# A build-time planner gets PSUM places and DMA queue times; filter products merged; x loads held

## The chip, the cores and the metric

One core of a Trainium2 chip. The metric is the device time of one execution in microseconds (us), less is better. The kernel before takes 312.05 us (median of three runs, 311.57 to 312.36).

The core has a matrix engine (PE, whose weight loads are the row PEld), two evacuating engines (DVE, the vector engine, and ACT, the scalar engine), POOL (GpSimd) and SP (the sync engine); POOL and SP here mainly issue DMAs. Each engine runs its own instructions strictly in order and waits on semaphores.

## The reference

Eight batches of 3200 x 256 values pass a global filter and then a gated unit:

```python
X = np.fft.rfft(x, axis=1)
y = np.fft.irfft(X * (filt_r + 1j * filt_i)[None], n=3200, axis=1)
xp = np.concatenate([np.zeros((B, 4, D)), y], axis=1)
gate_pre = sum(conv_w[k] * xp[:, k:k + S, :] for k in range(5))
out = (1 / (1 + np.exp(-gate_pre)) * (y @ w_val)) @ w_out
```

Input and output are float32; the kernel works in bf16 and fp16 with float32 accumulation.

## The kernel before

The length 3200 is split into 100 x 32, so that both transforms are two short matrix stages with a transposition between them. Every batch goes through the same pieces. The names are those of the planner's tasks, and the number of pieces per batch stands behind each.

- lx (8): POOL issues the load of a part of x (200 KB by the profile's list of issues) into one of ten buffers, converting to bf16 (line 168).
- s1 (8): PE, first transform stage (line 434). so (8): its evacuation from PSUM, on ACT or DVE.
- t (4): DVE transposes 32 x 32 blocks, tile `tt` (line 453). All eight so must be done.
- s2 (7): PE, second stage (line 463); xs (7): its evacuation.
- z (2 x 7): DVE multiplies xs by the real and by the imaginary filter part, `za` and `zb` (line 481).
- ia (7): PE, first inverse stage (line 494); ue (7): its evacuation into `u`.
- For batch 0, k (4): DVE transposes `u` into `vt` (line 535). For the other batches SP writes `u` to DRAM (wr, 7, line 517) and reads it back turned (lv, 8, lines 527 and 528).
- ib (8): PE, second inverse stage (line 545); ye (8): its evacuation on ACT (line 554) into `yt`.
- cv, ga, vl, gv, op, oe, st (7 each): convolution on PE as products with diagonal matrices (line 576), sigmoid on ACT (line 586), value product on PE (line 595), gate times value on DVE (line 610), output product on PE (line 618), its evacuation into `o` on ACT or DVE, and the store issued by SP (line 633).

At the start the transform tables are computed (iota, sine), the filter is loaded in two halves by POOL (lines 228 to 234) and doubled onto other partitions by SP (line 259), and the diagonal matrices `dg_t` are made on DVE (line 410).

**The order.** Nothing is scheduled at run time. The class `Plan` runs once when the kernel is built. Every piece is a task with costs for the engines that can do it, a rank, and tasks that it depends on; counted rooms (buffers) are taken and given back. `Plan.run` steps through an imagined time: whenever an engine is free, the ready task with the lowest rank goes next. PE changes between 64x64 and full tiles carry a penalty `stay`, and a task that both ACT and DVE could do carries `lean` on DVE. The list it returns is the order in which the instructions are emitted, and so the order in which each engine runs them. Its costs decide nothing but that order; on the chip each instruction waits for what it really needs.

PSUM is four tiles of [128, 1024] float32 from a pool that hands them out in turn:

```python
    def psum():
        return pp.tile([128, 1024], FP32, name="ps", tag="ps")
```

The plan counts them as one room (`ps=4`). x loads have the DMA queue as a task of 1.35 each ("DQ"), the spill and the stores have only fixed landing times.

Of the kernel before, what the change touches and what calls it, by code (L numbers as in the profile page):

```python
# [19 lines left out]
NM = 13  # L20
NV = 4 * NS
TURN = (0,)
RC = 4
# [4 lines left out]
MAGIC = 12582912.0  # L28


class Plan:
# [3 lines left out]
    def __init__(self, room, stay=1.0, lean=0.0):  # L35
        self.tasks, self.room, self.stay = {}, dict(room), stay
        self.lean = lean

    def add(self, name, engines, rank, deps, emit, take=(), give=(), land=0.0, mode=None):
        self.tasks[name] = dict(engines=engines, rank=rank, deps=deps, emit=emit, take=take,  # L40
                                give=give, land=land, mode=mode)

    def run(self):
# [8 lines left out]
        mode = None  # L52
# [4 lines left out]
        while left:  # L57
            gives.sort()
            while gives and gives[0][0] <= now + 1e-9:
                for pool in gives.pop(0)[1]:  # L60
                    self.room[pool] += 1
            best = None
            for n in ready:
# [23 lines left out]
            for p in t["take"]:  # L87
                self.room[p] -= 1
            if e == "PE":
                if t["mode"] != mode:  # L90
                    cost += 0.1
                mode = t["mode"]
            end = now + cost
            free[e] = end
            if t["give"]:
                gives.append((end + 0.1, t["give"]))
            for u in users.get(n, ()):
                need[u] -= 1
                ready_at[u] = max(ready_at[u], end + 0.1 + t["land"])
                if need[u] == 0:  # L100
                    ready.add(u)
            order.append((t["emit"], e))
# [5 lines left out]
def kernel(  # L108
# [36 lines left out]
    fr_t = cpool.tile([128, 2, NM, D], BF16, name="fr_t")  # L145
    fi_t = cpool.tile([128, 2, NM, D], BF16, name="fi_t")
# [5 lines left out]
    pp = ctx.enter_context(tc.tile_pool(name="ps", bufs=4, space=bass.MemoryType.PSUM))  # L152
# [6 lines left out]

    def psum():  # L160
        return pp.tile([128, 1024], FP32, name="ps", tag="ps")

    st = {}
# [39 lines left out]
    def pool_setup():  # L203
# [18 lines left out]
        for m0, m1 in FCUT:  # L222
            nm = m1 - m0
            for f, dst in ((filt_r, fr_t), (filt_i, fi_t)):
# [24 lines left out]
    def sp_setup():  # L249
# [5 lines left out]
        for m0, m1 in FCUT:  # L255
            for dst in (fr_t, fi_t):
                for t in range(2):
                    p = 64 * t
                    nc.sync.dma_start(out=dst[p + 32:p + 64, :, m0:m1, :],
                                      in_=dst[p:p + 32, :, m0:m1, :])  # L260
# [146 lines left out]
    def diag():  # L407
        for r in range(2):
            rows = slice(64 * r, 64 * r + 64)
            V.tensor_tensor(  # L410
                dg_t[rows].rearrange("p h k j -> p (h k) j"),
                g["ident"][rows, 64 * r:64 * r + 64].unsqueeze(1)
                .to_broadcast((64, 2 * K, 64)),
                g["cw"][rows].rearrange("p h k -> p (h k)").unsqueeze(2)
                .to_broadcast((64, 2 * K, 64)), op=ALU.mult)

    NGB, NOB = 3, 3
# [58 lines left out]
    def zed(b, u, which, e):  # L476
        m0, nm = UCH[u]
        xs_ = st["XS", b, u]
        z = zpool.tile([128, 2, 2 * D], BF16, name="za" if which == 0 else "zb")
        f = (fr_t, fi_t)[which]  # L480
        (nc.vector if e == "DVE" else nc.gpsimd).tensor_tensor(  # L481
            z[:, :, 0:nm * D], xs_[:, :, 0:nm * D],
            f[:, :, m0:m0 + nm, :].rearrange("p h m d -> p h (m d)"), op=ALU.mult)
        st["Z", b, u, which] = z

    def inva(b, u):
        m0, nm = UCH[u]
        zz = [st.pop(("Z", b, u, w)) for w in range(2)]
        ps = psum()
        for a in range(nm):  # L490
            for w, tab in enumerate((a_t, b_t)):
                for t, h in ((0, 0), (1, 1), (0, 1), (1, 0)):
# [4 lines left out]
                        rhs=zz[w][rows, h, D * a:D * a + D],  # L497
# [132 lines left out]
    def store(b, c):  # L630
# [7 lines left out]
    plan = Plan(dict(ps=4, xt=NXT, so=1, t=1, xs=3, za=3, zb=3, u=1, e=2, v=1, y=2, g=NGB,  # L638
                     gv=NGB, o=NOB), stay=1.5, lean=2)
# [4 lines left out]

    for b in range(B):
        t0 = NCH * b
        for j in range(NCH):
            if b:
                add(f"lx{b},{j}", {"POOL": 0.6}, t0 + j - 9, ["pool"],
                    lambda e, b=b, j=j: load_x(b, j), take=("xt",), land=1.5)  # L650
                add(f"dx{b},{j}", {"DQ": 1.35}, t0 + j - 9, [f"lx{b},{j}"], None, land=2.0)
            dep = [f"dx{b},{j}"] if b else [f"x0{j}", "cfa"]
            dep = dep + ([f"s1{b},{j - 1}"] if j else [])
            add(f"s1{b},{j}", {"PE": 0.45}, t0 + j, dep, lambda e, b=b, j=j: s1(b, j),
                take=("ps",) + (("so",) if j == 0 else ()), give=("xt",), mode=0)
            add(f"so{b},{j}", two(0.93, 1.14), t0 + j, [f"s1{b},{j}"],
                lambda e, b=b, j=j: so(b, j, e), give=("ps",))
        for q in range(4):
            add(f"t{b},{q}", {"DVE": 1.14}, t0 + NCH + 1.5, [f"so{b},{j}" for j in range(NCH)]
# [3 lines left out]
        for u, (m0, nm) in enumerate(UCH):  # L663
            r = t0 + NCH + 1 + u
            half = 0 if m0 + nm <= FCUT[0][1] else 1
            add(f"s2{b},{u}", {"PE": 0.14 * nm}, r, ["wa"] + [f"t{b},{q}" for q in range(4)]
                + ([f"s2{b},{u - 1}"] if u else []),
                lambda e, b=b, u=u: s2(b, u), take=("ps", "xs", "za", "zb"),
                give=("t",) if u == len(UCH) - 1 else (), mode=1)
            add(f"xs{b},{u}", two(0.13 + 0.4 * nm, 0.04 + 0.55 * nm), r, [f"s2{b},{u}"],  # L670
                lambda e, b=b, u=u: xs(b, u, e), give=("ps",))
            for w in range(2):
                add(f"z{w}{b},{u}", {"DVE": 0.06 + 0.27 * nm}, r, [f"xs{b},{u}", f"fl{half}"] + (
                    [f"z0{b},{u}"] if w else []),
                    lambda e, b=b, u=u, w=w: zed(b, u, w, e), give=("xs",) if w else ())
            add(f"ia{b},{u}", {"PE": 0.25 * nm}, r + 1.5, [f"z0{b},{u}", f"z1{b},{u}", f"te{u // 2},1", f"pd{b}"],
                lambda e, b=b, u=u: inva(b, u), take=("ps",), give=("za", "zb"), mode=1)
            add(f"ue{b},{u}", two(0.13 + 0.4 * nm, 0.04 + 0.55 * nm), r + 1.5, [f"ia{b},{u}", f"pd{b}"],
                lambda e, b=b, u=u: ue(b, u, e), give=("ps",))
        turned = b in TURN  # L680
        every = [f"ue{b},{u}" for u in range(len(UCH))]
        add(f"pd{b}", {"POOL": 1.2} if turned else {"none": 0.0}, t0 + NCH - 2,
            ["pool"] + ([f"pd{b - 1}"] if b else []),
            lambda e, b=b: pad(b), take=("u",) if turned else ("u", "e"))
        if turned:
            for q in range(4):
                add(f"k{b},{q}", {"DVE": 1.14}, t0 + NCH + 13, every
# [3 lines left out]
        else:  # L691
            for u in range(len(UCH)):
                r = t0 + NCH + 1 + u
                add(f"wr{b},{u}", {"SP": 0.45}, r + 1.5, [f"ue{b},{u}"],
                    lambda e, b=b, u=u: wr(b, u))
                add(f"wl{b},{u}", {"none": 0.0}, r + 1.5, [f"wr{b},{u}"], None, land=3.0)
            add(f"wd{b}", {"none": 0.0}, r + 1.5, [f"wl{b},{u}" for u in range(len(UCH))], None,
                take=("v",), give=("u",))
            for j in range(NCH):
                add(f"lv{b},{j}", {"SP": 0.8}, t0 + NCH + 13 + j, [f"wd{b}"],  # L700
                    lambda e, b=b, j=j: lv(b, j), land=3.5)
        for j in range(NCH):
            r = t0 + NCH + 11.5 + j
            got = f"k{b},3" if turned else f"lv{b},{j}"
            add(f"ib{b},{j}", {"PE": 0.37}, r, [got, "cim"] + ([f"ib{b},{j - 1}"] if j else []),
                lambda e, b=b, j=j: ib(b, j),
                take=("ps",) + (("y",) if j == 0 else ()),
                give=(("v",) if turned else ("v", "e")) if j == NCH - 1 else (), mode=0)
            add(f"ye{b},{j}", {"ACT": 0.77}, r, [f"ib{b},{j}"], lambda e, b=b, j=j: ye(b, j),
                give=("ps",))  # L710
        add(f"ha{b}", {"POOL": 0.2}, t0 + NCH + 11.5, [f"ye{b},0"], lambda e, b=b: halo(b))
        for c in range(NB):
            r = t0 + NCH + 18 + c * 1.3
            f = width(c) / BLK
            add(f"cv{b},{c}", {"PE": 1.03 * f + 0.05}, r,
                [f"ye{b},{j}" for j in range(NCH)] + [f"ha{b}", "dg"],
                lambda e, b=b, c=c: conv(b, c), take=("ps", "g"), mode=1)
            add(f"ga{b},{c}", {"ACT": 0.77 * f + 0.16}, r, [f"cv{b},{c}"],
                lambda e, b=b, c=c: gate(b, c), give=("ps",))
            add(f"vl{b},{c}", {"PE": 0.86 * f}, r, [f"cv{b},{c}"] + ([f"vl{b},{c - 1}"] if c else []),  # L720
                lambda e, b=b, c=c: val(b, c),
# [75 lines left out]
```

## Time and profile before

| | us |
|---|---|
| median of the runs shown | 312.05 |
| the profiled execution, its own time | 313.69 |
| its span, first to last instruction | 311.8 |
| busy PE / DVE / ACT / POOL | 267.2 / 260.7 / 252.8 / 57.8 |
| mean granted PE clock | 0.967 of full |
| DMA bytes | 67.45 MB, mean 216 GB/s |

The profile is one execution. Times that follow are us from the span's start. "Busy" of neighbouring instructions overlaps a little, so that the distance from one start to the next is shorter than the duration shown. A row "A <- B" under the waits says that engine A stood idle until B had finished. In the table of stretches every line gives the start and end, the length, the busy time of PE, PEld, DVE, ACT and POOL with the number of instructions in brackets, the granted clock, the mean busy share of the 16 DMA engines and GB/s. In the timeline a line gives the start, the time taken, the engine, the kernel's line, the operation, what it writes and reads, and in brackets the idle time before it and what ended it.

### The profile page before, as it was taken

How to read it: one execution, taken by the hardware profiler on the slowest of the kernel's cores; microseconds unless marked ns; L12 is line 12 of the kernel's file. 1: busy time of each engine (PE TensorE's matmuls, PEld its weight loads, DVE VectorE, ACT ScalarE, POOL GpSimd, SP SyncE). 2: the span in 40 equal slices, each digit the busy share in tenths (PEclk: the TensorE clock that was granted, in tenths of full speed). 3: DMA queues.
4: the chain of work that ended last, by engine and by line, in shares of the span. 5: the costliest groups of instructions: out<-in, count | busy, mean ns of one | idle time of the engine just before them, and what ended most of it. 6: DMA issues, size and time to landing. Idle time of an engine off the chain costs nothing.

```text
span 311.8 us, 8932 instructions
## 1 busy us (share of the span) xinstructions
PE 267.2 (86%) x3684; PEld 160.2 (51%) x3684; DVE 260.7 (84%) x339; ACT 252.8 (81%) x294; POOL 57.8 (19%) x119
## 2 busy tenths in 40 slices
PE   2815770886999999999999999999999999999992
PEld 0204130254466746665666566656665666666551
DVE  7698689899799989998999899989998985553342
ACT  3945580699699999999999999999999889688762
POOL 8676572230212022102210220000000000000000
PEclk9999996598999999999999999999999999999997
DMA  6999999597799979998999799776566875754444
GB/s 96 178 168 183 209 124 177 76 179 197 179 241 242 269 224 238 311 285 240 249 313 272 226 248 312 245 243 210 177 237 221 244 264 204 260 204 185 167 177 180
DMA packets 53209, 67.45 MB, mean 216 GB/s; under 512 B 7792, under 2 KB 34032, under 8 KB 53168
## 3 DMA queue, kind: packets, MB, share of 16 engines
q1 hardware_dynamic: 41264, 51.79, 50.2%
q0 software_dynamic: 11904, 15.08, 30.7%
q8 instruction: 29, 0.48, 0.6%
q14 instruction: 12, 0.10, 0.1%
HBM read 42.08 MB, written 38.14 MB: 257 GB/s over the span
## 4 chain that ended last, share of the span: by engine, by line
PE 60%; DVE 14%; ACT 9%; DMA 9%; issue 4%; POOL 2%; DVEq 0%; ACTq 0%; POOLq 0%
PE ps L576 17%; PE ps L595 12%; PE ps L618 11%; PE ps L434 7%; PE ps L494 6%; DMA xt<-in_x_dram 6%; DVE gv L610 5%; PE ps L545 4%; DMA fi_t<-in_filt_i_dram 4%; ACT yt L554 3%; PE ps L463 3%; DVE so L427 2%; ACT o L425 2%; ACT u L425 2%; DVE vt L535 2%
## 5 line engine op out<-in xcount | busy, mean ns | idle before, releaser
L610 DVE TENSOR_TENSOR gv<-ps,gt 128x1024 bf16<-128x1024 f32 (+1 forms) x56 | 61.3, 1105 | 27.7 <-ACT gt L586 14.0
L576 PE MATMUL ps<-yt,dg_t 64*64 64x512 bf16 (+1 forms) x1120 | 65.1, 361 | 2.3 <-ACT yt L554 1.6
L586 ACT ACTIVATE gt<-ps 128x1024 bf16<-128x1024 f32 (+1 forms) x56 | 52.1, 934 | 11.0 <-PE ps L576 8.4
L554 ACT ACTIVATE yt<-ps 128x800 bf16<-128x800 f32 x64 | 53.6, 843 | 6.6 <-PE ps L545 5.9
L168 POOL DMA_DIRECT2D xt<-in_x_dram x64 | 35.5, 557 | 119.9 <-PE ps L434 110.3
L434 PE MATMUL ps<-xt,cf_t 100*128 100x512 bf16 x128 | 46.2, 450 | 11.8 <-DMA xt<-in_x_dram 8.7
L618 PE MATMUL ps<-wo_t,gv 128*128 128x256 bf16 x400 | 52.3, 273 | 1.4 <-DVE gv L610 1.2
L595 PE MATMUL ps<-yt,wv_t 128*128 128x512 bf16 (+1 forms) x224 | 52.4, 357 | 0.0
L425 ACT ACTIVATE so<-ps 128x1024 bf16<-128x1024 f32 x40 | 40.8, 1024 | 10.3 <-PE ps L434 7.5
L425 ACT ACTIVATE u<-ps 128x1024 bf16<-128x1024 f32 (+1 forms) x46 | 43.2, 958 | 2.9 <-PE ps L494 2.7
L425 ACT ACTIVATE o<-ps 128x1024 f32<-128x1024 f32 (+1 forms) x44 | 40.8, 938 | 5.2 <-PE ps L618 4.4
L618 PEld LDWEIGHTS <-gv 128*128 128x128 bf16 x400 | 35.8, 97 | 17.0 <-DVE gv L610 7.0
L425 ACT ACTIVATE xs<-ps 128x1024 bf16<-128x1024 f32 (+1 forms) x32 | 29.5, 931 | 17.4 <-PE ps L463 17.2
L576 PEld LDWEIGHTS <-dg_t 64*64 64x64 bf16 x1120 | 32.0, 107 | 22.0 <-issue 6.2
L453 DVE STREAM_TRANSPOSE tt<-so 128x1024 f32<-128x1024 f32 x32 | 38.5, 1227 | 0.6 <-ACT so L425 0.6
L463 PE MATMUL ps<-tt,w_t 64*64 64x256 bf16 x416 | 23.2, 297 | 18.4 <-DVE tt L453 17.5
L481 DVE TENSOR_TENSOR zb<-xs,fi_t 128x1024 bf16<-128x1024 bf16 (+1 forms) x56 | 35.4, 642 | 0.6 <-DMA fi_t<-in_filt_i_dram 0.4
L481 DVE TENSOR_TENSOR za<-xs,fr_t 128x1024 bf16<-128x1024 bf16 (+1 forms) x56 | 35.2, 643 | 0.7 <-ACT xs L425 0.5
L427 DVE CAST so<-ps 128x1024 bf16<-128x1024 f32 x24 | 28.8, 1219 | 7.5 <-PE ps L434 7.5
L545 PEld LDWEIGHTS <-vt 104*128 104x128 bf16 (+1 forms) x512 | 28.9, 98 | 10.6 <-issue 1.9
L545 PE MATMUL ps<-ci_t,vt 104*128 104x100 f16 (+1 forms) x512 | 33.3, 209 | 0.6 <-DVE u L427 0.5
L494 PE MATMUL ps<-za,a_t 64*64 64x256 bf16 x416 | 28.5, 290 | 2.9 <-DVE za L481 1.6
(93 smaller groups left out, 212.3 us busy)
## 6 DMA issues: line engine op xcount, KB each, us to landing
out_dram<-o SPq DMA_DIRECT2D x48, 512.0 KB
xt<-in_x_dram POOLq DMA_DIRECT2D x64, 200.0 KB, 6.4
escr<-u SPq DMA_DIRECT2D x42, 256.0 KB
vt<-escr SPq DMA_DIRECT2D x56, 192.0 KB
out_dram<-o SPq DMA_DIRECT2D x8, 128.0 KB
escr<-u SPq DMA_DIRECT2D x7, 128.0 KB
vt<-escr SPq DMA_DIRECT2D x56, 16.0 KB
fr_t<-fr_t SPq DMA_DIRECT2D x2, 224.0 KB
```

The source lines that it names most:

```text
L425: nc.scalar.activation(dst, src, AF.Copy, **kw)
L434: nc.tensor.matmul(ps[:, 512 * h:512 * h + 512], lhsT=cf_t[0:L].rearrange("p h c i -> p (h c i)"), rhs=xv[:, DQ // 2 * h:DQ // 2 * h + DQ ...
L453: nc.vector.transpose(dst, src)
L481: (nc.vector if e == "DVE" else nc.gpsimd).tensor_tensor(z[:, :, 0:nm * D], xs_[:, :, 0:nm * D], f[:, :, m0:m0 + nm, :].rearrange("p h m d ...
L494: nc.tensor.matmul(ps[64 * h:64 * h + 64, 512 * t + D * a:512 * t + D * a + D], lhsT=tab[rows, h, m0 + a, :], rhs=zz[w][rows, h, D * a:D * ...
L545: nc.tensor.matmul(ps[:, o:o + L], lhsT=v[rows, RC * j + a, 128 * dh:128 * dh + 128], rhs=ci_t[rows, way, :], start=True, stop=True)
L554: nc.scalar.activation(y[:, :, H:H + N].rearrange("p h (a r) -> p h a r", r=R)[:, :, :, RC * j:RC * j + RC], ps[:, :].rearrange("p (h n) - ...
L576: nc.tensor.matmul(ps[64 * dh:64 * dh + 64, 512 * r:512 * r + w], lhsT=dg_t[rows, dh, k, :], rhs=y[rows, dh, BLK * c + k:BLK * c + k + w], ...
L586: nc.scalar.activation(g[:, :, 0:w], two_banks(ps, w), AF.Sigmoid)
L595: nc.tensor.matmul(ps[:, 512 * eh:512 * eh + w], lhsT=wv_t[:, dh, 128 * eh:128 * eh + 128], rhs=y[:, dh, H + BLK * c:H + BLK * c + w], sta ...
L610: nc.vector.tensor_tensor(o, i0, i1, op=ALU.mult)
L618: nc.tensor.matmul(ps[:, D * a:D * a + D], lhsT=gv_[:, eh, 128 * a:128 * a + 128], rhs=wo_t[:, eh, :], start=(eh == 0), stop=(eh == 1))
```

## The change

The planner gets explicit PSUM places, a DMA queue that all transfers share, new costs and new ranks; the kernel gets a merged filter product, diagonal matrices made on ACT, five output buffers and a hold before the later x loads. The order on every engine changes nearly everywhere.

1. PSUM is one tile with four places; a task takes a free place chosen by the plan, which is emitted as written, and the evacuating task gives it back.
2. Spill writes, spill reads and stores pass the task engine "DQ" with costs of their own (0.38 per column, 0.6, 1.2; an x load 1.15). "DQ" takes the task that was ready first and alternates between x loads and the rest.
3. Ranks: `at(stage, n, b)` = 8b + LAG + STEP x n, and FIRST for batch 0, in place of hand-set offsets; `stay` 17.5 and `lean` 12 in place of 1.5 and 2.
4. One z of up to 2048 elements replaces za and zb: xs is read twice through a step of 0, both filter parts stand in one tile `f_t`.
5. `dg_t` is made by ten small ACT instructions, early; the inverse tables (`cid`) wait for batch 0's last t.
6. A one-column copy on POOL reads the last filter column (`hold`); the x loads of batches 1 to 7 and the weight loads depend on it.
7. Output buffers: 3 to 5.

```diff
-    def add(self, name, engines, rank, deps, emit, take=(), give=(), land=0.0, mode=None):
+    def add(self, name, engines, rank, deps, emit, take=(), give=(), land=0.0, mode=None,
+            ps=0, free=()):
...
+    def places(self, n):
+        if n == 0:
+            return []
+        if n == 1:
+            alone = [p for p in self.slots if p ^ 1 not in self.slots]
+            return (alone or self.slots)[:1] or None
...
-                if any(self.room[p] < 1 for p in t["take"]):
+                if self.places(t["ps"]) is None or any(self.room[p] < 1 for p in t["take"]):
...
+                        if e == "DQ":
+                            key = (ready_at[n] + (1e4 if t["mode"] == turn else 0.0), 0.0)
...
+            t["slots"] = self.places(t["ps"])
+            for p in t["slots"]:
+                self.slots.remove(p)
...
+            done = end + SEM.get(e, 0.1)
+            back = list(t["give"]) + [p for o in t["free"] for p in self.tasks[o]["slots"]]
...
+    f_t = cpool.tile([128, 2, 2, NM, D], BF16, name="f_t")
...
+    ps_all = pp.tile([128, 4, 1024], FP32, name="ps")
...
     def psum():
-        return pp.tile([128, 1024], FP32, name="ps", tag="ps")
+        return ps_all[:, st["slots"][0], :]
...
-    def diag():
...
+    def diag(h):
+        for k in range(K):
+            nc.scalar.activation(dg_t[:, h, k, :], g["j2"][:, 0, :], AF.Copy,
+                                 scale=g["cw"][:, h, k:k + 1])
+
+    def gate_loads():
+        hold = g1.tile([128, 1], BF16, name="hold")
+        nc.gpsimd.tensor_copy(hold[...], f_t[:, 1, 1, NM - 1, 0:1])
+
+    NGB, NOB = 3, 5
...
+    def zed(b, u):
+        m0, nm = UCH[u]
+        z = zpool.tile([128, 2, 2, 2 * D], BF16, name="z")
+        nc.vector.tensor_tensor(
+            z[:, :, :, 0:nm * D],
+            st.pop(("XS", b, u))[:, :, 0:nm * D].unsqueeze(1)
+            .to_broadcast((128, 2, 2, nm * D)),
+            f_t[:, :, :, m0:m0 + nm, :].rearrange("p w h m d -> p w h (m d)"), op=ALU.mult)
...
+    def dma(name, us, rank, dep, give=(), land=2.0):
+        add(name, {"DQ": us}, rank, dep, None, land=land, mode=0)
+        add(name + "+", {"none": 0.0}, rank, [name], None, give=give)
...
+        def at(stage, n=0, b=b, t0=t0):
+            return t0 + LAG[stage] + (FIRST.get(stage, 0) if b == 0 else 0) + STEP.get(stage, 1) * n
...
-                add(f"lx{b},{j}", {"POOL": 0.6}, t0 + j - 9, ["pool"],
+                add(f"lx{b},{j}", {"POOL": 0.6}, at("lx", j), ["hold"],
                     lambda e, b=b, j=j: load_x(b, j), take=("xt",), land=1.5)
-                add(f"dx{b},{j}", {"DQ": 1.35}, t0 + j - 9, [f"lx{b},{j}"], None, land=2.0)
+                add(f"dx{b},{j}", {"DQ": 1.15}, at("lx", j), [f"lx{b},{j}"], None, land=2.0, mode=1)
...
-    add("cid", {"DVE": 4.5}, 9, ["wd"], lambda e: ci_dve())
+    add("cid", {"DVE": 4.5}, 13, ["t0,3"], lambda e: ci_dve())
...
-    add("dg", {"DVE": 3.2}, 10, ["t0,3"], lambda e: diag())
+    for h in range(2):
+        add(f"dg{h}", {"ACT": 1.1}, 10, ["ey"], lambda e, h=h: diag(h))
+    add("hold", {"POOL": 0.2}, 0, ["fl1", "pd0"], lambda e: gate_loads())
```

What the new plan puts out for the first batches, against the old one (PE's order, piece by piece, from batch 0's fifth ia on):

```
before: ia0.4 s11.5 s20.6 s11.6 ia0.5 s11.7 ia0.6 s21.0 s12.0 s21.1 s12.1 ib0.0 s12.2 s21.2 ... ib0.7 ia1.5 ia1.6 cv0.0
after:  ia0.4 ia0.5 ia0.6 s11.0 s11.1 ... s11.7 ib0.0 ib0.1 ... ib0.7 s12.0 s21.0 s12.1 s21.1 s12.2 s21.2 s12.3 cv0.0
```

On DVE the four k of batch 0 stand ahead of the four t of batch 1; before they alternated.

More of the change, by code (lines that the diff above doesn't have):

```diff
@@ L51, in run @@
         free = {}
-        mode = None
+        mode = turn = None
         gives = []
@@ L223, in pool_setup @@
             nm = m1 - m0
-            for f, dst in ((filt_r, fr_t), (filt_i, fi_t)):
+            for f, dst in ((filt_r, f_t[:, 0]), (filt_i, f_t[:, 1])):
                 for t in range(2):
@@ L474, in xs @@
         st["XS", b, u] = xs_
-    def zed(b, u, which, e):
+    def zed(b, u):
         m0, nm = UCH[u]
[L478 to L484, printed above, removed]
+        z = zpool.tile([128, 2, 2, 2 * D], BF16, name="z")
[4 more added lines that the diff above has]
+            f_t[:, :, :, m0:m0 + nm, :].rearrange("p w h m d -> p w h (m d)"), op=ALU.mult)
+        st["Z", b, u] = z
     def inva(b, u):
         m0, nm = UCH[u]
-        zz = [st.pop(("Z", b, u, w)) for w in range(2)]
+        z = st.pop(("Z", b, u))
         ps = psum()
@@ L662 @@
                 give=("so",) if q == 3 else ())
[L663 to L679, printed above, removed]
@@ L685 @@
         if turned:
             for q in range(4):
-                add(f"k{b},{q}", {"DVE": 1.14}, t0 + NCH + 13, every
+                add(f"k{b},{q}", {"DVE": 1.87}, at("k"), [f"ue{b},{u}" for u in range(len(UCH))]
                     + ([f"k{b},{q - 1}"] if q else []),
@@ L691 @@
         else:
[L692 to L698, printed above, removed]
+            add(f"wd{b}", {"none": 0.0}, at("ue"), [f"wq{b},{u}+" for u in range(len(UCH))],
+                None, take=("v",), give=("u",))
@@ L732 @@
-    add("pool", {"none": 0.0}, -100, [], None, land=22.0)
-    add("wts", {"POOL": 8.0}, 8.5, ["pool"], lambda e: load_w())
+            add(f"cv{b},{c}", {"PE": 1.08 * f}, at("cv", c),
+                [f"ye{b},{j}" for j in range(NCH)] + [f"ha{b}", "dg0", "dg1"],
+                lambda e, b=b, c=c: conv(b, c), ps=1, take=("g",), mode=1)
+            add(f"ga{b},{c}", {"ACT": 0.77 * f + 0.16}, at("ga", c), [f"cv{b},{c}"],
+                lambda e, b=b, c=c: gate(b, c), free=[f"cv{b},{c}"])
+            add(f"vl{b},{c}", {"PE": 0.87 * f}, at("vl", c),
+                [f"cv{b},{c}"] + ([f"vl{b},{c - 1}"] if c else []), lambda e, b=b, c=c: val(b, c),
+                ps=1, take=("gv",), give=("y",) if c == NB - 1 else (), mode=0)
```

162 lines of the change are left out of this document (90 added, 72 removed).

## The prediction

> **What bounds the kernel now.** I read four views in this order: the slices (where are engines idle), the stretches (which engine fills a batch), the waits (who holds the idle ones), the timeline (what the holder does). "b.n" below is batch b, piece n; s1, so, t, s2, xs, z, ia, ue, ib, ye, cv, ga, vl, gv, op, oe are the planner's task names.
>
> ```profile
> PE   2815770886999999999999999999999999999992
> DVE  7698689899799989998999899989998985553342
> ACT  3945580699699999999999999999999889688762
> PEclk9999996598999999999999999999999999999997
> ```
>
> A slice is 7.8 us. The first 78 us are full of holes on PE and ACT, from slice 11 to 30 all three engines are full, and the last ten slices leave only PE full.
>
> ```profile
> 46.00:56.00 10.00, 0.32 (x8) 0.19 (x8) 10.00 (x8) 0.15 (x1) 3.09 (x6) 0.64 0.95 163
> 108.00:139.70 31.70, 30.89 (x454) 19.63 (x451) 30.36 (x35) 29.89 (x36) 4.54 (x9) 1.00 0.93 262
> 139.70:171.30 31.60, 30.93 (x456) 19.66 (x454) 30.13 (x35) 29.84 (x36) 4.54 (x9) 1.00 0.96 267
> 265.00:308.00 43.00, 41.30 (x509) 24.56 (x507) 19.78 (x19) 30.35 (x35) 0.10 (x1) 1.00 0.53 197
> ```
>
> Columns: stretch, length, then busy us of PE, PEld, DVE, ACT, POOL, granted clock, DMA share, GB/s. The reader is to see three regimes: 46 to 56, DVE alone works; 108 to 234, one batch per 31.6 us with PE, DVE and ACT all over 94% busy and the DMA engines at 0.93 to 0.96; from 265 PE alone.
>
> ```profile
> PE ps L463 <- DVE tt L453: 17.5, 2, 10.2
> ACT xs L425 <- PE ps L463: 17.2, 4, 10.2
> ```
>
> Ten of these us are the hole at 46, and the timeline names it:
>
> ```profile
> 45.70 1.25 DVE L453 STREAM_TRANSPOSE tt<-so 128x1024 f32<-128x1024 f32 x1 [0.59 <-ACT so L425]
> 46.87 1.87 DVE L535 STREAM_TRANSPOSE vt<-u 128x1024 f32<-128x1024 f32 x1
> 48.64 1.20 DVE L453 STREAM_TRANSPOSE tt<-so 128x1024 f32<-128x1024 f32 x1
> ```
>
> DVE turns batch 1's input (L453) and batch 0's output (L535) alternately, eight transposes in 12 us, and PE and ACT can start neither batch until nearly all are done.
>
> **Prices from rows.** Busy times of neighbours overlap, so I take start-to-start distances in the full stretch: DVE evacuation of 1024 elements or a gv 1.14 us, tt 1.16, vt 1.79, za or zb 0.60 (0.31 for the half piece); ACT evacuation 0.92, yt 0.73; PE s1 0.45, s2 0.23, ia 0.44, ib 0.36, cv 1.08, vl 0.87, op 0.88 a piece, about 0.1 at each change between 64x64 and full tiles. These rows give it:
>
> ```profile
> 179.18 1.28 DVE L481 TENSOR_TENSOR za<-xs,fr_t 128x1024 bf16<-128x1024 bf16 x2
> 180.38 0.68 DVE L481 TENSOR_TENSOR zb<-xs,fi_t 128x1024 bf16<-128x1024 bf16 x1
> 180.98 1.22 DVE L610 TENSOR_TENSOR gv<-ps,gt 128x1024 bf16<-128x1024 f32 x1
> 198.52 0.38 DVE L481 TENSOR_TENSOR za<-xs,fr_t 128x512 bf16<-128x512 bf16 x1
> 198.82 1.23 DVE L453 STREAM_TRANSPOSE tt<-so 128x1024 f32<-128x1024 f32 x1
> ```
>
> **The head (to the end of batch 1's tt; before: 55.6).** The built order shows what moves. DVE: the ci tables (4.6 us, 13.8 to 18.4 before) now stand behind batch 0's tt, dg_t (1.6) leaves for ACT as ten small instructions; none such is in the trace, and 128x128 ACT rows with and without a scale operand (0.16 and 0.36) bound them at 1.6 to 3.6 us, I take 2.6, before the seventh so. Batch 0's tt then ends near 22 instead of 24. That gain is worth nothing: the first z needs the filter, and zb waited for it until 27.85. One z now needs both filter parts, so z0.0 starts there, not at 25.8. The second filter half was issued until 24.8, its SP copies from 28.44; I take 34 for its landing (32.5 to 36). The hold on POOL reads its last column; behind it in POOL's queue stand ten x loads, the weights and every later x load, and s1 of batch 1, in PE's order behind ia0.6, waits for them. Batch 0's eight x loads took 1.45 to 14.06, 12.6 us: batch 1's last x at 46.6, its so at 48. Meanwhile z0.3 to z0.6 run 34 to 38.2, ue to 39.3, and the four vt stand first on DVE: 46.5. So tt runs 48 to 52.7. I take **53** (51 to 55): 2.6 us earlier, and vt is no longer behind it (before to 57.4). Cover: the held loads hide behind the vt; a hold landing at 38 would show its 4 us in full. [...]
>
> **The middle (batch 1's tt to batch 7's; before 55.6 to 236.6: 181 us).** DVE's order between these marks, counted: evacuations and gv 81 of 1.14 become 73; half evacuations 1 become 7 (0.57), one o of 0.33 comes; 72 za/zb of 0.60 and 12 of 0.31 become 36 z and 6 half z; one vt (1.79) leaves; 24 tt and 4 small gv (0.35) stay. A z of 2048 is in no row: 1024 costs 0.60 and 512 0.31, a straight line gives 1.18; no gain would be 1.20, and I take 1.18 (half z 0.60). Sums: 170.8 us before, 162.9 after; z gives only 0.8 of that, the moved evacuations and vt the rest. [...] ACT takes over: between the last yt of batches 0 and 6 its work grows from 165.5 to 176.5 us (so 23 to 41, u 36 to 30, o 32 to 29), in 189 us before, so it has room. PE does 144.4 us and 92 tile changes there, 153.6 in all, 160.3 before.
> PSUM places: the pool handed its four tiles out in turn, so a piece waited for the tile of four pieces earlier even where another was free; the plan now names a free one. No row shows this wait apart: DVE idles 1.3 to 1.5 us a batch in the full stretch. The places gain between nothing (DVE stays at 29.9/31.6 = 94.6%) and all of it; I take 96.5%. The middle is 162.9/0.965 = **168.8 us** (162.9 to 172.2 by these bounds).
> Five output buffers cost and gain nothing: before an o the engines waited 10.1 us for PE and 0.3 for a DMA. SP issues the same DMAs in another order; on its queue a store still stands behind spill writes that wait for their u (SP waited 54.6 us for o on ACT and 35.2 for u on ACT), and the o buffers already hide that. By the issue lists and sizes about 43 MB fall into the middle, 255 GB/s, below the 267 that the stretch at 139.7 carried.
>
> **The tail.** From s2 of batch 7 PE has 63.4 us and 32 changes left before: 66.6 in 70.8 us (237.2 to 308). After: 68.8 and 16 changes, 70.4, since some of batch 4's cv, vl and op come later. At the same rate that is **74.8 us**. Cover: PE has no second use for a hole here; DVE's 46 us (40.7 before) fit in with room.
>
> **Sum.** 53 + 168.8 + 74.8 + 3.8 (the last store, 308.0 to 311.8 before) = 300.4 of span, against 311.8. The profiled execution took 313.69, 1.89 outside its span; the median of the runs shown, 312.05, lies 1.64 under it. 300.4 + 1.89 - 1.64 = 300.65: **301 us**.
>
> **Rivals.**
> (B) Better packing: with all idle gone and the head at 51, 51 + 162.9 + 73 + 3.8 + 0.25, so 291. For: three balanced engines. Against: before never reached it in any batch. [...]
> (C) The work leaves DVE and turns into waits of in-order queues, as DVE's 2.73 us for a late x at 35.86 before: the middle at 91.5%, 178 us in place of 168.8: 310.
> (D) Slower: DMA takes over. While x still streams, a batch moves 8.4 MB; at 28.1 us that asks 300 GB/s. If the queues cannot hold over 267, batches 2 to 6 keep 31.6 us: 5 x 3.5 = 17.5 more, 318. It decides from about 285 GB/s needed over a whole batch. For: share 0.96. Against: two 8 us stretches carried 311 and 316 GB/s.
> (E) The merged z loses its rate, reading xs twice at step 0. The f32 row of 1664 elements at 1.89 us says 2.33 for 2048: 48 x 1.15 us and more on DVE, about 356. Nothing in the trace has this form in bf16. [...]
>
> **Chances.** Forecast 0.52 (294 to 306), B 0.17, C 0.19, D 0.08, E 0.04. The range 289 to 311 leaves out D, E and the edges of B and C. About 0.3% (1 us) is what a measurement can tell from no change. C reaches to 312: I give 0.13 of it to faster and 0.06 to same; faster 0.82, same 0.06, slower 0.12.
>
> **What would show it.** Right: tt of batch 1 done at 51 to 55 with vt ahead of it, batch 7's tt done near 222, PE full from there, z rows spaced about 1.18. Wrong: x of batch 1 landing after 50; holes before ib behind vt loads with GB/s flat at 267 (D); z over 2 us (E); PE holes after tt7 (tail priced too low); an ACT row full while DVE idles.

## The result and the profile after

The changed kernel takes 308.01 us (median of four runs, 306.52 to 308.76). Its ratio to the kernel before is 0.9865, 95% interval 0.9826 to 0.9905; a second set of runs gave 0.9844 (0.9784 to 0.9903). Ratios leave disturbed executions out, medians do not, so that the two can differ a little. The time fell by 4 us where 11 were forecast.

I cut both spans at the same two marks, the end of batch 1's last tt and the end of batch 7's last tt, as the prediction did.

| us | head | middle | rest of span | span |
|---|---|---|---|---|
| before | 55.6 | 180.9 | 75.2 | 311.8 |
| forecast | 53 | 168.8 | 78.6 | 300.4 |
| changed kernel | 54.2 | 173.9 | 78.2 | 306.3 |

The head is 1.2 us and the rest 0.4 us from the forecast. The middle is 5.1 us too long: this is the miss. (The forecast's rest was counted from the first s2 of batch 7, which before started 0.6 us behind the mark; counted so, it is 77.9 in the changed kernel.)

The slices of the changed kernel (7.66 us each):

```profile
PE   2831789889988898999699999998999999999993
DVE  7688997889999899998399999989999985455442
ACT  3864879999799899997689999999889977786663
PEclk9999955999999999999999999999999999999998
```

The hole that PE and ACT had at 46 to 56 is filled. A new one has come in slice 19 (counted from 0, 145.5 to 153.2): DVE 3, PE 6, ACT 6.

Stretches of the changed kernel (columns as before: stretch, length, busy PE, PEld, DVE, ACT, POOL, clock, DMA share, GB/s):

```profile
46.00:56.00 10.00, 9.12 (x91) 5.95 (x90) 8.17 (x8) 9.85 (x13) 7.54 (x15) 0.69 0.98 137
108.00:139.70 31.70, 29.72 (x382) 18.26 (x377) 31.69 (x29) 30.85 (x36) 7.85 (x15) 1.00 0.96 245
139.70:171.30 31.60, 28.10 (x473) 18.50 (x467) 25.55 (x26) 24.67 (x31) 0.66 (x2) 1.00 0.82 250
265.00:302.50 37.50, 35.57 (x449) 22.81 (x452) 18.89 (x19) 26.26 (x29) 0.00 (x0) 1.00 0.53 203
```

Where before one stretch was like the other, DVE is now full from 108 and then loses 6 us out of 31.6; the last line shows PE alone full, as before.

DVE around the head's mark, from the timeline of the changed kernel:

```profile
29.23 3.49 DVE L512 TENSOR_TENSOR z<-xs,f_t 128x2048 bf16<-128x2048 bf16 x3 [0.93 <-DMA f_t<-in_filt_i_dram]
34.66 4.20 DVE L512 TENSOR_TENSOR z<-xs,f_t 128x2048 bf16<-128x2048 bf16 x4 [0.45 <-ACT xs L458]
40.49 7.36 DVE L568 STREAM_TRANSPOSE vt<-u 128x1024 f32<-128x1024 f32 x4
49.55 4.62 DVE L486 STREAM_TRANSPOSE tt<-so 128x1024 f32<-128x1024 f32 x4 [1.70 <-ACT so L458]
```

The four vt stand first, then the four tt, ended at 54.2; in between DVE waits 1.70 us for the last so of the held x. Three z in 3.49 us, the last lasting 1.21, are 1.14 us from one start to the next.

The new hole, first in the waits of 130 to 175, then in the chain of waits of 120 to 180 (start, length, what), then in SP's DMA issues:

```profile
DVE u L460 <- DMA out_dram<-o: 5.0, 1, 5.0
ACT u L458 <- DMA out_dram<-o: 1.9, 1, 1.9
```

```profile
140.58 0.02 issue
140.60 10.74 DMA escr<-u
...
151.65 1.24 DVE u L460
```

```profile
127.73 12.42 SPq L666 DMA_DIRECT2D out_dram<-o  x6
140.60 0.38 SPq L550 DMA_DIRECT2D escr<-u  x1
...
151.35 0.29 SPq L561 DMA_DIRECT2D vt<-escr  x1
```

There is one tile u. Its last piece of batch 3 is written to DRAM by a transfer issued at 140.60, behind six stores of o issued from 127.73 on the same queue. It landed at 151.34, and until then no piece of batch 4 could be put into u. The waits name "out_dram<-o", the transfer that ended just then; the chain names the one that matters. In the run e10 below, with the same u and the same order, the row names it too:

```profile
148.22 1.23 DVE L460 CAST u<-ps 128x1024 bf16<-128x1024 f32 x1 [4.90 <-DMA escr<-u]
```

In the kernel before no u waited for a DMA. There SP issued the same batch's last four writes like this:

```profile
130.99 2.08 SPq L633 DMA_DIRECT2D out_dram<-o  x2
133.64 6.20 SPq L517 DMA_DIRECT2D escr<-u  x4
140.51 1.27 SPq L633 DMA_DIRECT2D out_dram<-o  x2
141.96 0.59 SPq L527 DMA_DIRECT2D vt<-escr  x1
142.64 0.73 SPq L528 DMA_DIRECT2D vt<-escr  x1
```

The last of the four went out at 139.5, 3.4 us behind the third, and the second reader, which is the one that is late in the changed kernel, was issued at 142.64. In the changed kernel the last write stands 14.6 us behind the one before it, with the six stores between.

### The profile page after: what moved, and what is told of

The parts are those of the page before. It is cut to its first block, busy times and chain, and to the rows that moved or that the text cites. A ratio compares the mean times of both kernels' runs of the same rounds, so it can differ in the third digit from the quotient of the medians.

```text
span 306.3 us, 8876 instructions
## 1 busy us (share of the span) xinstructions
PE 263.4 (86%) x3658; PEld 160.3 (52%) x3684; DVE 255.6 (83%) x284; ACT 254.3 (83%) x301; POOL 58.0 (19%) x120
## 4 chain that ended last, share of the span: by engine, by line
PE 41%; DVE 20%; DMA 14%; ACT 12%; issue 6%; POOL 4%; SPq 0%; DVEq 0%; ACTq 0%; POOLq 0%
PE ps L609 12%; PE ps L651 10%; PE ps L628 9%; DVE xs L460 6%; DVE z L512 6%; DMA xt<-in_x_dram 5%; PE ps L578 4%; DVE gv L643 4%; DMA escr<-u 4%; ACT yt L587 3%; PE ps L527 3%; ACT so L458 3%; DVE u L460 3%; DMA f_t<-in_filt_r_dram 2%; PE ps L467 2%
## 5 line engine op out<-in xcount | busy, mean ns | idle before, releaser
L643 DVE TENSOR_TENSOR gv<-ps,gt 128x1024 bf16<-128x1024 f32 (+1 forms) x56 | 60.7, 1100 | 24.4 <-PE ps L628 17.5
L512 DVE TENSOR_TENSOR z<-xs,f_t 128x2048 bf16<-128x2048 bf16 (+1 forms) x56 | 62.1, 1140 | 1.5 <-DMA f_t<-in_filt_i_dram 0.9
L609 PE MATMUL ps<-yt,dg_t 64*64 64x512 bf16 (+1 forms) x1120 | 60.7, 354 | 0.6 <-ACT yt L587 0.5
L458 ACT ACTIVATE so<-ps 128x1024 bf16<-128x1024 f32 x55 | 53.7, 1044 | 7.9 <-PE ps L467 5.6
L587 ACT ACTIVATE yt<-ps 128x800 bf16<-128x800 f32 x64 | 51.4, 852 | 7.0 <-PE ps L578 6.8
L628 PE MATMUL ps<-yt,wv_t 128*128 128x512 bf16 (+1 forms) x198 | 50.5, 354 | 1.8 <-DVE xs L460 0.3
L458 ACT ACTIVATE u<-ps 128x1024 bf16<-128x1024 f32 (+1 forms) x35 | 35.4, 1022 | 7.2 <-PE ps L527 5.4
L527 PE MATMUL ps<-z,a_t 64*64 64x256 bf16 x416 | 28.3, 288 | 13.1 <-DVE z L512 9.0
L460 DVE CAST xs<-ps 128x1024 bf16<-128x1024 f32 (+1 forms) x27 | 30.7, 1156 | 0.5 <-PE ps L496 0.4
L458 ACT ACTIVATE xs<-ps 128x1024 bf16<-128x1024 f32 (+1 forms) x29 | 27.2, 974 | 4.1 <-PE ps L496 4.1
L628 PEld LDWEIGHTS <-wv_t 128*128 128x128 bf16 x224 | 18.7, 97 | 19.8 <-issue 5.6
```

Of the source, the lines that this page charges most:

```text
L458: nc.scalar.activation(dst, src, AF.Copy, **kw)
L460: nc.vector.tensor_copy(dst, src)
L512: nc.vector.tensor_tensor(z[:, :, :, 0:nm * D], st.pop(("XS", b, u))[:, :, 0:nm * D].unsqueeze(1) .to_broadcast((128, 2, 2, nm * D)), f_t[ ...
L587: nc.scalar.activation(y[:, :, H:H + N].rearrange("p h (a r) -> p h a r", r=R)[:, :, :, RC * j:RC * j + RC], ps[:, :].rearrange("p (h n) - ...
L609: nc.tensor.matmul(ps[64 * dh:64 * dh + 64, 512 * r:512 * r + w], lhsT=dg_t[rows, dh, k, :], rhs=y[rows, dh, BLK * c + k:BLK * c + k + w], ...
L628: nc.tensor.matmul(ps[:, 512 * eh:512 * eh + w], lhsT=wv_t[:, dh, 128 * eh:128 * eh + 128], rhs=y[:, dh, H + BLK * c:H + BLK * c + w], sta ...
```

## The experiments

All experiments but e8 and e9 keep the order of the changed kernel on every engine. "Middle" is the stretch between the two marks and "rest" what follows it, from the one profiled execution of each run. The same kernel gave 173.9 and 175.6 there, so differences under 2 us in it say little by themselves.

**e1: pieces of u.**

```diff
+    st = {"UA": upool.tile([128, 32, D], BF16, name="u")}
...
-        st["U", b] = upool.tile([128, 32, D], BF16, name="u")
+        st["U", b] = st["UA"]
```

> One u tile is kept for all batches instead of a new one per batch, so that a piece of u waits only for the spill write of the same piece of the batch before; the order on every engine is that of the changed kernel (308.0). In its profile DVE stood 5.0 us and ACT 1.9 us before a u at 151.6, until batch 4's last spill write, issued at 140.6, had landed at 151.3. Theory 1, this single wait is what the middle lost against the forecast: DVE has no gap there, tt of batch 7 ends near 223 instead of 228.1, and the time is 302 to 304. Theory 2, the DMA engines are the bound (their share was 0.9 or more up to 150): the time comes back as waits for x or vt, 306.5 to 308. Theory 3, PE is the other bound: it lost only 2.6 us at 150 to 160, so 305 to 306, with PE full and DVE still idle.

(The write is that of batch 3, and the u that waited batch 4's; I had the batch wrong by one, here and in the texts of e7.) Measured: 305.5 us, ratio 0.9794 (0.9767 to 0.982); middle 171.2. This is 2.5 us less than the changed kernel, theory 3's size. On DVE, e1's timeline:

```profile
143.86 2.36 DVE L643 TENSOR_TENSOR gv<-ps,gt 128x1024 bf16<-128x1024 f32 x2 [0.44 <-PE ps L628]
148.70 1.23 DVE L460 CAST u<-ps 128x1024 bf16<-128x1024 f32 x1 [2.48 <-PE ps L527]
```

and on PE:

```profile
144.77 3.44 PE L609 MATMUL ps<-yt,dg_t 64*64 64x512 bf16 x60
148.04 0.28 PE L527 MATMUL ps<-z,a_t 64*64 64x256 bf16 x4
```

The DMA wait is gone, and 2.48 of its 5.0 us are still there: PE's list has three cv (60 matmuls) ahead of the ia whose result DVE waits for. The plan knew of u's wait, which may be why they stand there; this was not shown (e9, planned without that wait, has a gap there too). So the spill wait cost some 2.5 us, and this version beats both kernels.

**e7 and e15: half stores**, on the changed kernel and on e1.

```diff
-            out=out[b, BLK * c:BLK * c + w, :].rearrange("(p r) d -> p (r d)", p=128),
-            in_=o[:, 0:w // 128 * D])
+            out=out[b, BLK * c:BLK * c + w, :].rearrange("(p r) d -> p (r d)", p=128)[:, 0:w // 256 * D or D],
+            in_=o[:, 0:w // 256 * D or D])
```

> Same order and the same u tile per batch as the changed kernel, but each store writes only half of its o to DRAM, so half of the output is left out; this takes some 13 MB from the queue in front of the spill writes. Theory 1, the spill write of batch 4 landed 10.7 us after its issue because of the stores issued from 130.3 to 140.2 ahead of it on the same queue: it lands within 5 us, the gap of DVE at 146.6 shrinks to the 2.5 us that PE's order leaves, and the time is that with the pieces of u, 305 to 306. Theory 2, the DMA engines set the pace elsewhere too: below 303. Theory 3, the spill write is slow by itself: 308.

> The version with one u tile, and every store writing half of its o (half of the output left out; 13 MB of 67 less). Half stores on the changed kernel gave 305.2, as much as the u tile alone. If DMA still sets something in the middle or the tail: 300 to 303. If the spill wait was all that DMA cost: 304.5 to 306.

Measured: e7 305.24, ratio 0.9775 (0.9729 to 0.982), middle 171.4, and the same 2.48 us of DVE waiting for PE at 149.77. e15 304.65, 0.9771 (0.9733 to 0.981), middle 172.6. Half the bytes ahead of the spill write cure the wait as the u tile does, and together they give no more: the stores matter through this one wait, and with the engines' work as it is nothing else in the time hangs on the bytes stored. The write still took up to 8.2 us in e7 (issued 141.25, its reader issued 149.47), not the 5 I expected; the x loads running beside it were not varied, so what else slows it is open. The other runs bear it out: every profile with the one u per batch, five output buffers and whole stores has a wait of 3.2 to 5.1 us of DVE for a DMA at this u, and none of those with the single u tile or with half stores has one.

**e2: PSUM places in turn.**

```diff
-        return ps_all[:, st["slots"][0], :]
+        return pp.tile([128, 1024], FP32, name="ps", tag="ps")
```

> Same order on every engine as in the changed kernel, but PSUM's four places are handed out in turn again, not by the plan. The prediction put the places at 0 to 3.4 us of DVE's idle time (94.6% against 96.5%) and took 3.4: the time would be 311.4. If the gain of the places is nothing: 308. If the plan's order rests on them (a piece is sent to a place that comes free out of turn), several us more: 313 to 320, with PE waiting for evacuations of an older place.

Measured: 310.62, ratio 0.9928 (0.9899 to 0.9958). The places are worth 0.6 to 0.8%, some 2 to 2.6 us, with intervals that just touch those of the changed kernel; I had taken 3.4. Where they lie is not settled: e2's middle, 175.3, lies between the 173.9 and 175.6 of the changed kernel.

**e3: three output buffers**, the order kept.

```diff
-    opool = ctx.enter_context(tc.tile_pool(name="ost", bufs=NOB))
+    opool = ctx.enter_context(tc.tile_pool(name="ost", bufs=3))
```

> Same order, but three output buffers instead of five. The prediction: five gain nothing, 308. Rival: the changed kernel issues four stores from 130.3 to 140.2 into a full queue, so the fourth o would wait for the first store, and with it whatever stands behind that o on DVE or ACT: 310 to 314, with o waiting for out_dram.

Measured: 307.75, 0.9874 (0.9839 to 0.9909): no difference in the time, as predicted, but not because nothing happens. In its profile an o waits for a store five times, 3.9 us in all (at 131.92 for 0.57 us; the longest, 1.35, at 300.27), and no o of the changed kernel does. The spill write is done sooner: its reader was issued at 149.37 instead of 151.35, and the u at 149.57 waited 2.97 us for PE, not for a DMA. Five buffers also let stores run ahead of the write that u needs, so a gain and a loss may have cancelled here.

**e4: no hold.**

```diff
-        nc.gpsimd.tensor_copy(hold[...], f_t[:, 1, 1, NM - 1, 0:1])
+        nc.gpsimd.memset(hold[...], 0.0)
```

> Same order, but the small POOL instruction ahead of the x loads no longer reads the filter (it writes a constant), so the loads of batch 1 are issued from about 27.5 instead of 35.0. The prediction: the hold is hidden behind the four vt up to 1.7 us (tt of batch 1 waited that long for so at 49.55), so 306.3 to 308, with tt of batch 1 starting at about 47.9. Rival: the x loads now run beside the filter's copies (28 to 34 us) and delay the second filter half, z, ue and the vt by 1 to 4 us: 309 to 312.

Measured: 311.66, 0.9988 (0.9961 to 1.0014): without the hold the whole change is worth nothing that can be measured. The rival was right. DVE in e4:

```profile
32.74 1.22 DVE L460 CAST u<-ps 128x1024 bf16<-128x1024 f32 x1
38.89 3.50 DVE L512 TENSOR_TENSOR z<-xs,f_t 128x2048 bf16<-128x2048 bf16 x3 [4.94 <-DMA xt<-in_x_dram]
```

The z that needs the second filter half starts 4.2 us later (38.89 against 34.66); vt and tt move with it (tt of batch 1 ends at 56.7). The row names an x load, which ended just then; what z reads is the filter's last copy, which SP issued at 31.9 here and at 31.6 with the hold. So the copy was not issued much later but took longer: POOL had issued nine x loads by 33.5, and from 28 to 34 the DMA engines moved 200 GB/s instead of 135.

**e8: the hold alone, in the kernel before.**

```diff
     def load_x(b, j):
+        if (b, j) == (1, 0):
+            hold = g1.tile([128, 1], BF16, name="hold")
+            nc.gpsimd.tensor_copy(hold[...], fi_t[:, 1, NM - 1, 0:1])
```

> The kernel before (312.1), its order unchanged on PE, DVE, ACT and SP, with only the hold put in front of batch 1's x loads on POOL (the zeroing of u's unused columns goes ahead of it). Without the hold the changed kernel took 3.6 us more, so if the hold is a gain in itself (the filter's copies run undisturbed): 308.5 to 310. Rival: it pays only in the new order. In the old one s1 of batch 1 stands between batch 0's ia on PE, so PE waits for held x with ia behind it: 314 to 320, with PE waiting for x up to about 42 us.

Measured: 317.1, ratio 1.0163 (1.0109 to 1.0218). Its waits:

```profile
PE ps L437 <- DMA xt<-in_x_dram: 13.6, 4, 6.9
```

Before, that row was 8.7 us. The old list has s1 of batch 1 among the ia of batch 0, so held x stops the ia behind it, and batch 1's tt ends at 59.1 instead of 55.6. Of these two orders, the hold is a gain only in the one that first finishes batch 0's ia.

**e5: z in two instructions.**

```diff
-        nc.vector.tensor_tensor(
-            z[:, :, :, 0:nm * D],
...
+        for w in range(2):
+            nc.vector.tensor_tensor(
+                z[:, w, :, 0:nm * D], xs_[:, :, 0:nm * D],
+                f_t[:, w, :, m0:m0 + nm, :].rearrange("p h m d -> p h (m d)"), op=ALU.mult)
```

> Same order as the changed kernel, but every z is two instructions again, each over one filter part. The prediction put the gain of the single z at 0.8 us (1.18 against 1.20 a piece). In the changed kernel a z starts 1.13 to 1.14 after the one before, so 42 full pieces of the middle are worth 2.5 to 2.8 us of DVE time. If DVE alone sets the middle: 310.5 to 311. If PE sets as much of it, as the experiment with the pieces of u says: 308 to 309.5. Never faster than 307.5.

Measured: 310.02, 0.9927 (0.9896 to 0.9958), some 2 us over the changed kernel, with intervals that just touch. But in the profile the middle is 174.0 with 2.3 us more DVE work (165.0 busy against 162.7), so the middle did not take it up; that execution was later in the head (tt of batch 1 ended at 55.8, after 4.93 us in which DVE waited for so). Where the 2 us lie is therefore not settled.

Taken out one at a time, the hold (3.7 us), the places (2 to 2.6) and the single z (some 2) make about 8 us, twice what the whole change gained. So these parts do not add up to the whole, and what the new order by itself gives or costs no run shows.

**c_after: the changed kernel again.**

> The changed kernel again, beside the others: 308.0, between 306.5 and 309, for every theory.

Measured: 309.02, ratio 0.9844 (0.9784 to 0.9903).

**e9: planned anew for pieces of u**, on e1, with all ranks changed too.

```diff
-                [f"ia{b},{u}"], lambda e, b=b, u=u: ue(b, u, e), free=[f"ia{b},{u}"])
+                [f"ia{b},{u}"] + ([f"wq{b - 1},{u}+" if b > 1 else "k0,3"] if b else []),
+                lambda e, b=b, u=u: ue(b, u, e), free=[f"ia{b},{u}"])
```

> One u tile kept for all batches, as in the first experiment (305.5), and the planner now told so: a piece of u waits for the spill write of the same piece of the batch before, and the ranks are chosen anew for that. In the first experiment DVE still stood 2.5 us at 148.7 because PE's list had three cv in a row ahead of the first ia of batch 4. If that list is what is left: 302 to 304, with no gap of DVE over 1.5 us between the ends of tt of batches 1 and 7. If other waits take its place (PE and DMA are nearly full as well): 305 to 307.

Measured: 309.69, 0.9924 (0.9887 to 0.9961): worse than e1. A gap of 2.23 us before a u at 149.5 remains, and PE now waits 4.2 us for vt loads. All ranks changed, so what made it slower than e1 is open.

**What holds the middle: lighter engines.** e10, e13: the convolution with four of its five taps (PE lighter), on the changed kernel and on e1. e11: half of every z (DVE lighter), on the changed kernel. e12: half of the gate's sigmoid (ACT lighter), on e1. e14, e16, e17, e18: these together, on e1.

```diff
-        for k in range(K):
+        for k in range(1, K):
...
-        nc.scalar.activation(g[:, :, 0:w], two_banks(ps, w), AF.Sigmoid)
+        nc.scalar.activation(g[:, 0, 0:w], ps[:, 0:w], AF.Sigmoid)
...
-            z[:, :, :, 0:nm * D],
+            z[:, :, 0, 0:nm * D],
```

> The changed kernel with four of the five taps of every convolution, so the convolution is not the reference's; 16 of 20 matmuls a piece, 0.22 us less PE work in each cv, 12 us in all, of which 4.9 us stand behind the end of batch 7's tt. Order and everything else unchanged (308 to 309). If DVE sets the middle, as the prediction has it, only the tail becomes shorter: 303 to 304.5. If PE sets the middle as much as DVE: 298 to 301, and near 296 if PE alone does.

> The changed kernel with only the first half of every z computed and used twice by ia, so the filter is applied to half of the frequencies; 0.57 us less on DVE for each of 48 pieces, some 24 us in the middle; the same matmuls and the same order. If DVE's work times its utilisation sets the middle, it falls until ACT is the bound (176.5 us of work between the last yt of batches 0 and 6, in 181 to 189): 298 to 301. If PE's list and the waits set as much: 303 to 306. The spill wait at 140 to 151 stays in either case, since it hangs on the queue.

> The version with one u tile (305.5; its stretch from the end of batch 1's tt to that of batch 7 took 171.2), and the sigmoid of only the first half of every piece, used twice: about 0.4 us less on ACT for each of 56 pieces, some 22 us in all and 13 in that stretch; half of the gate is left out. If ACT, to which the change moved work, has become what sets the middle: the stretch falls to 160 to 165 and the time to 296 to 300. If the three engines hold one another up in turn, so that no single one sets it: 303 to 305.5. PE and DVE do the same work in the same order.

> The version with one u tile, and four of five taps in the convolution (0.22 us less PE work in each cv; the convolution is not the reference's). On the changed kernel the same cut made the stretch between the tt of batches 1 and 7 no shorter (174.1 against 173.9), with the spill wait still in it. If PE sets the middle once that wait is gone: the stretch falls from 171.2 by 5 to 7, the time to 294 to 297. If the engines hold one another up: the tail alone gains, 300.5 to 303.

> Both cuts of the two runs before together (half of the gate's sigmoid, four of five taps): PE and ACT lighter, DVE as it is. If the engines hold one another up in turn, the two together gain more than the sum of each alone, and DVE comes to 97% or more of the stretch: 163 to 168, and 292 to 298 in all. If the list and its dependences (the one so, tt, u, vt buffers) set it whatever the engines' work: 299 to 302.

> One u tile, half of every z, and four of five taps: DVE and PE lighter, ACT as it is. Alone, half z on the changed kernel left the stretch between the tt of batches 1 and 7 at 171.0, four taps with one u tile at 169.7, half the gate at 170.7, taps and gate at 168.1. If ACT is what is left then: 169 or more, and 300 in all. If the engines hold one another up in pairs: 162 to 167, 294 to 298.

> One u tile, half of every z and half of the gate's sigmoid: DVE and ACT lighter, PE's work and order as they are. If PE's list, with the waits that every switch of stage costs it, sets the middle: 169 or more, 304 to 305 in all. If it is the pair DVE and ACT, which empty PSUM: 160 to 166, 295 to 300.

> One u tile and all three cuts: DVE, ACT and PE lighter by some 18, 11 and 7 us in the stretch. If the engines hold one another up, all three together gain what none gains alone: 158 to 163, and 289 to 294 in all. If it is the DMA traffic or the chain of single buffers (so, tt, u, vt): 166 to 168, and 298 to 299.5 as with taps and gate.

| run | lighter | time | ratio, interval | middle | rest |
|---|---|---|---|---|---|
| e10 | PE | 304.72 | 0.9771, 0.9724 to 0.9819 | 174.1 | 74.6 |
| e11 | DVE | 307.46 | 0.9843, 0.9793 to 0.9893 | 171.0 | 78.2 |
| e12 on e1 | ACT | 305.63 | 0.9798, 0.975 to 0.9845 | 170.7 | 78.1 |
| e13 on e1 | PE | 300.75 | 0.9633, 0.9586 to 0.9681 | 169.7 | 74.5 |
| e14 on e1 | PE, ACT | 299.52 | 0.9623, 0.9554 to 0.9692 | 168.1 | 74.5 |
| e16 on e1 | PE, DVE | 299.81 | 0.9624, 0.9556 to 0.9692 | 168.2 | 74.5 |
| e17 on e1 | DVE, ACT | 302.62 | 0.9716, 0.9676 to 0.9756 | 168.5 | 77.9 |
| e18 on e1 | all three | 296.67 | 0.9511, 0.9461 to 0.9561 | 166.6 | 73.6 |

The whole middle as one stretch, in the changed kernel, in e11 and in e18:

```profile
54.17:228.08 173.91, 160.44 (x2338) 97.53 (x2356) 162.69 (x153) 158.86 (x183) 22.23 (x46) 1.00 0.87 241
```

```profile
54.03:225.01 170.98, 160.93 (x2355) 97.27 (x2356) 144.54 (x153) 158.70 (x183) 22.14 (x46) 1.00 0.90 245
```

```profile
54.58:221.23 166.65, 153.05 (x2205) 93.18 (x2223) 143.89 (x153) 147.22 (x183) 22.21 (x45) 1.00 0.92 252
```

e11 has 18 us less DVE work there, and its ratio, 0.9843, lies with the 0.9865 and 0.9844 of the changed kernel: in that kernel DVE's work alone does not set the time. Of its middle's 2.9 us the spill gap is 1.8, 3.2 instead of 5.0 us. On e1, PE's work alone gives the middle 1.5 us (e13) and ACT's 0.5 (e12), no more than two profiles of one kernel differ. Half of z alone was not run on e1, so it is open whether DVE alone counts once the spill wait is gone: e17 adds only this cut to e12 and gains 3 us, e16 adds it to e13 and gains 1. Two lighter engines give the middle 3 us, all three, with 38 us of busy time taken out (8 of PE, 18.6 of DVE, 11.6 of ACT, against e1), 4.6. A mutual hold-up by work would have given far more in e18; I had expected 158 to 163. In e18 no engine is over 92% busy, and its chain of waits for 56 to 220 has as its longest pieces

```profile
83.82 9.67 DMA vt<-escr
93.51 6.93 DMA vt<-escr
...
138.55 11.50 DMA escr<-u
```

so the spill's way to DRAM and back has become a part of it: the view puts 11.9% of the stretch down to vt<-escr and 7.0% to escr<-u, though PE's lines together still have more. Whether this, the bytes moved (252 GB/s) or PE's list is the floor near 167 was not tried by a run; it stays open.

## Why the prediction was wrong in size

**What held.** The forecast was faster, 308 lies in the range, and the places of the change came out as worked. Head: hold at 34.5 (34 forecast), vt done at 47.9 (46.5), tt at 54.2 (51 to 55); the ten dg instructions took 2.48 us (2.6). DVE's work in the middle: 162.7 us busy (162.9 counted from start to start; before, the two measures gave 172.1 and 170.8). Output buffers: nothing in the time (e3). Rest: 78.2 (78.6); e10 and e13 show that PE sets it, since PE was busy 3.7 and 4.1 us less behind the mark and the rest became 3.6 us shorter in both.

**The step that failed** is "The middle is 162.9/0.965 = 168.8 us". It made DVE's work over a utilisation the middle. The work was right and the utilisation was not: DVE was busy 162.7 of 173.9 us, 93.5%, less than the 95.1% of the kernel before. The runs showed two things in its place.

First, a wait that the prediction took for hidden: it said of the spill writes behind stores that "the o buffers already hide that". They hide o, not u. With one u tile, the next batch's u waits for the last write, and the new order put six stores ahead of it. e1 and e7 remove it in two ways and gain the same 2.5 to 2.8 us; the other half of the gap is a wait for PE. In e1 the middle is 171.2 and DVE busy 94.9% of it, so some 2.7 of the 5.1 us are found.

Second, the rule itself. Taking 18 us off DVE left the time of the changed kernel where it was (e11), so its middle is not DVE's work over a constant share; the share fell with the work, to 84.5% in e11. What sets the other 2.4 us is open. The chain of waits, which the prediction did not read, could have warned. Before and after, by engine, from the page:

```profile
PE 60%; DVE 14%; ACT 9%; DMA 9%; issue 4%; POOL 2%; DVEq 0%; ACTq 0%; POOLq 0%
```

```profile
PE 41%; DVE 20%; DMA 14%; ACT 12%; issue 6%; POOL 4%; SPq 0%; DVEq 0%; ACTq 0%; POOLq 0%
```

In the kernel before, PE carried the chain and DVE a seventh of it, though their busy shares were alike. PE's own count in the prediction fell from 160.3 to 153.6, by 6.7 us, and the middle by 7.0; that the one is the other's cause is argued, not shown, and with the chain now spread over PE, DVE and DMA a further 3.6 us less busy PE (e13 against e1) gave 1.5. Nor are the chain's shares a price: DVE has 20% of it after, and e11 took nothing off the time.

"ACT has room" was also read wrongly: its 176.5 us were set against the 189 us of the old window, which the forecast itself shortened. e12 shows that this did not decide, but the sentence bounded nothing.

**Terms that were mis-sized.** Places: 2 to 2.6 us, not 3.4. z: 1.14 us a piece, which reads xs again at a step of 0, where za and zb together had taken 1.20; not 1.18, and rival E, with 2.33, is out. The hold was priced as a risk hidden by the vt, and not as a gain; it is 3.7 us in this order and a loss of 5 in the old. The sum also left out the 0.6 us between the mark at 236.6 and the tail's start at 237.2.

**Rivals.** C, work turned into in-order waits, was nearest in kind: the middle fell between its 178 and the forecast. D is out: the changed kernel carried 284 GB/s from 78 to 108, over the 267 that D took as a cap. B did not come; that bandwidth kept it out was not shown: e1 moved 368 GB/s from 160 to 171.3, and whether as much can be held over a whole batch is open.

## What to carry to other kernels

When several in-order engines are all over 90% busy, do not take the work of one over a fixed share as the time. Read the chain of waits too, and try what a lighter engine gives before you build on it: here lighter work on one of them moved the middle by 3 us at most, and on all three by 4.6. For a buffer with one copy, follow what gives it back: if that is a DMA, what was issued before it on its queue can be on the path of the next use (10.7 us here), and tracking the tile by pieces took that wait away. A load held back for another's sake paid here only where PE's list had nothing urgent behind the held work: a gain of 3.7 us in the new order, a loss of 5 in the old.

## What the runs showed of the hardware

The granted clock has to be read together with the matmuls. In the changed kernel it was 0.62 from 36 to 46 us, 0.69 from 46 to 56 and 0.50 throughout 38.5 to 52.1. The stretches of e1, with the same list, show 1.00 from 36 to 56. But the matmuls of s1 there, first in the changed kernel, then in e1, then later in the changed kernel (count, shortest, median and longest in ns, first and last start), were as slow as with the low clock:

```profile
L467 PE MATMUL ps<-xt,cf_t x16: 586/628/632, 39.5 to 47.8; 100*128 100x512 bf16 x16
L467 PE MATMUL ps<-xt,cf_t x16: 582/628/628, 39.6 to 47.6; 100*128 100x512 bf16 x16
L467 PE MATMUL ps<-xt,cf_t x16: 382/382/395, 106.3 to 113.7; 100*128 100x512 bf16 x16
```

The clock record of e1's trace only starts at 51.3, so its 1.00 before that is no measurement. Batch 1's tt ended at 54.2 and 53.9, and what the low clock cost there no run shows. PE was busy for 12.65 us of the changed kernel's 13.6 us at 0.50.

A small transfer took long behind large ones: the last spill write of batch 3, of 128 KB, took 10.7 us while the DMA engines were busy with six stores of 512 KB and eight x loads of 200 KB. In a stretch in which POOL issued no x load the same engines moved 322 GB/s (158 to 168 of the changed kernel).
